# Query and key of two of eight batches transposed by DMA instead of VectorE

## The chip, the cores and the metric

The kernel runs on one core of one Trainium2 chip. The metric is the device time of one execution in microseconds (us); the median of three runs of the kernel before is 153.43 us (152.05 to 155.81). A core has five engines with a queue of instructions each: TensorE (PE, matrix products into PSUM; its weight loads are shown as PEld), VectorE (DVE), ScalarE (ACT), GpSimd (POOL) and SyncE (SP). POOL and SP also issue DMA transfers; all transfers run on the same 16 DMA engines. Each engine works through its own instructions in the order in which they were written, and waits on semaphores for the others.

## The reference

The inputs are `q`, `k` and `v`, each of 8 batches, 8 heads, 576 positions and 64 elements in float32, and the weights of a highway layer of width 512.

```python
rel = pos[:, None] - pos[None, :]
scores = q @ k.T / sqrt(64) + slope[h] * (-abs(rel))      # slope[h] = 2 ** -(h + 1)
scores = where((rel >= 0) & (rel < 128), scores, -1e9)    # causal window of 128
x = softmax(scores) @ v                                   # -> 4608 rows of 512 (8 heads x 64)
H = relu(x @ w_h);  T = sigmoid(x @ w_t + b_t)
out = T * H + (1 - T) * x
```

The output is float32, 4,608 rows of 512. Inside the kernels the products run on bfloat16, cast by the loading DMAs.

## The kernel before, in words

**Units and blocks.** Attention goes by units `(b, s, g)`: batch b (8), half of the heads s (2, four heads each), half of the positions g (2): 32 units. The highway layer goes by blocks of 128 output rows `(b, i)`, 36 in all: four per batch, and in each odd batch a fifth (`i == 4`) with the first 64 rows of two batches.

**The order is written out by hand.** The string `ORDER` (L26) holds one letter per step, and `by` (L56) says which unit, block or load each next use of a letter takes; a digit behind a letter is the PSUM bank. Every step's instructions stand in their engines' queues in exactly this order. `LOADS` (L18) is the order of the loads among themselves.

**Steps of a unit.** `L` issues a load from POOL (L126 to L144): a `t` load brings q or k of four heads of a batch, cast to bfloat16, as 128 rows of 1,152 elements; a `v` load brings 128 positions of v for 8 or 16 heads in pieces of 64 elements. A load's semaphore is one of eight in rotation, so that each issue also waits for the load eight places earlier. `T` (L188) transposes a `t` tile on DVE in 32x32 blocks of pairs of elements, so that the 64 elements of a head stand in 32 rows as two interleaved halves. `s` (L197) makes the scores of a unit from them: products over 32 rows, two of them (e = 0, 1) added up in PSUM for each head and place, with the tiles of four heads at rows 0, 32, 64 and 96. `e` is the exponential on ACT (L245), `m` the multiplication with a table of bias and mask on DVE (L250); for three units, `MASK_PE` (L23), TensorE adds the bias to the scores instead (L204). `p` multiplies with v (L261 to L282; the sum of the probabilities comes along as a 65th column), and `n` divides, on DVE (L295, L296).

**Steps of a block.** `x` transposes x on TensorE, `c` copies it out on ACT, `h` is the product with `w_h` (L331). `u` gives relu(h) - x on DVE, in one instruction out of PSUM (L346) or, for the blocks in `RELU_ACT` (L15), after a relu on ACT (`r`, L338) from SBUF (L343). `z` is the product with `w_t` plus a product of a matrix that is one in its first row with the bias tile (L354, L356); for the blocks in `BIAS_ACT` (L20) ACT writes the bias into PSUM first (`w`, L360) and `y` adds the product (L364). `a` is tanh of half of it on ACT (L369), turned into the sigmoid by `t` on ACT (L373) or, for blocks in `GATE_DVE` (L16), by `k` on DVE (L377). `g` multiplies on DVE (L382). `o` adds x on POOL (L386), or `q` on DVE (L391) for the blocks in `ADD_DVE` (L21). `d` stores from SP (L394). The tiles `uu`, `tt` and `ot` have four buffers each.

So POOL's queue holds the loads and the sums of L386 in one order, SP's the stores, and a step that waits holds up all that stands behind it on its engine.

Of the kernel before, what the change touches and what calls it, by code (L numbers as in the profile page):

```python
# [9 lines left out]
P = 128  # L10
NB, NS, NG = 8, 2, 2
NLD, NTR, NPB = 20, 12, 8

RELU_ACT = (0, 3, 5, 8, 9, 11, 12, 13, 17, 19, 20, 21, 26, 28)  # L15
GATE_DVE = (6, 7, 9, 15, 19, 23, 25, 26, 29, 32, 34)  # L16

LOADS = (0, 1, 3, 4, 6, 5, 2, 12, 11, 9, 13, 17, 10, 16, 8, 18, 7, 14, 21, 19, 15, 20, 22, 27, 26, 23, 25, 24, 29, 30, 31, 32, 33, 28, 34, 37, 39, 35, 40, 47, 38, 36, 43, 44, 45, 46, 48, 42, 41, 52, 56, 57, 50, 53, 58, 59, 51, 49, 55, 54)  # L18

BIAS_ACT = (8, 9, 14, 17, 20, 24, 30, 31, 32, 33, 34, 35)  # L20
ADD_DVE = (33, 35)  # L21

MASK_PE = (11, 14, 19)  # L23
# [3 lines left out]
    "SLLSSLLLTLLTLs0LTLeLLTLSms0Lp4LeLTLmLs0LTp6enLs0nLmx4Lex5Tp6cmcs0Lnz4eLTp6mas0tnz4eLh5mx"  # L27
    "6rh7cux5az6ucgtTp4oaSp6nLds0nLh4Th5eLx6x7uLrs0Tcz4Leumh5cmx6as0cuz7egTp4oh6anLtds0Lmrp4t"
    "Luez6ngz7gaoTtx6p4aLmdcs0x7eh6noTp4Ltds0cLnmh7euz4kw6gux5aos0Tch7eLdTp4Lynrs0akmp4w7eyug"
    "nh6oaTx4rs0LdtgLcgLp6gmx4Lz5cnex4oTp6cLds0unLz4eoTp6aLds0anoh5tTeh4dmz6rux7ah4kmcx5tp6uc"  # L30
    "gs0rnox5ez4TLdh6gLcmax7s0roTz5cw4Lgp6deuTyLts0naLaLgz4ueLTop6Tas0otdh5enh4dgux6oth7ucgx4"
    "w5dh6mctoyurTx4ap6dcms0z4euknh5agp6Ttos0th4neLduz6rmLLx7ap4mcs0np6egx4kh5nocs0ruLdx4gw5p"
    "6LmcyeuLnh4Tox6az7rmtLdp4ags0cgz7otneTz6odTx4aLds0cx5mah4w7uh6cgkeuyoup4gtds0maz6eonx7Tp"
    "4dcs0nh7eTh4h5autmp6rgs0uz5oenx4mdp6cs0uakz4engx5p6macs0onx4z5cdmeh4ggp6aoux5nh4odctz5kr"
    "mdw4h6gauox7tx5uycgdkh6gaocx4h7ucodw6p4utydnw7ygagow6p4aytnodh7agdtx6ox4uh5ckw7dh6gcuoyw"
    "5uygdaqh4akdgtuogdqd"
# [3 lines left out]
def lists():  # L40

    units = [(b, s, g) for b in range(NB) for g in range(NG) for s in range(NS)]
    blocks = []
    for b in range(NB):
        blocks += [(b, 0), (b, 1)] + ([(b, 4)] if b % 2 else []) + [(b, 2), (b, 3)]
    trs = [(b, s, w) for b in range(NB) for s in range(NS) for w in range(2)]
    loads = []
    for b in range(NB):
        n = 1 if b < 2 else 2
        vs = [("v", b, n, m) for m in range(5)] if b < 2 or b % 2 == 0 else []  # L50
        ts = [("t", b, s, w) for s in range(NS) for w in range(2)]
        if b == 0:
            loads += ts[:2] + vs[:1] + ts[2:] + vs[1:3] + [("w", 0), ("w", 1), ("w", 2)] + vs[3:]
        else:
            loads += ts[:2] + vs[:3] + ts[2:] + vs[3:]
    by = dict(L=[loads[i] for i in LOADS], T=trs, S=list(range(5)))  # L56
    by.update({k: units for k in "sepn"})
    by["m"] = [u for i, u in enumerate(units) if i not in MASK_PE]
    by["pe_mask"] = [units[i] for i in MASK_PE]
    by.update({k: blocks for k in "xchuzagod"})  # L60
    by["w"] = by["y"] = [blocks[i] for i in BIAS_ACT]
    by["z"] = [bk for i, bk in enumerate(blocks) if i not in BIAS_ACT]
    by["q"] = [blocks[i] for i in ADD_DVE]
    by["o"] = [bk for i, bk in enumerate(blocks) if i not in ADD_DVE]
    by["r"] = [blocks[i] for i in RELU_ACT]
    by["k"] = [blocks[i] for i in GATE_DVE]
    by["t"] = [bk for i, bk in enumerate(blocks) if i not in GATE_DVE]
    return by
# [3 lines left out]
def kernel(  # L72
# [35 lines left out]
    ft = ctx.enter_context(tc.tile_pool(name="ft", bufs=4))  # L108
    pp = ctx.enter_context(tc.tile_pool(name="ps", bufs=1, space=PSUM))
# [4 lines left out]
    PB = [cp.tile([P, 4, 448], BF16, name=f"p{i}") for i in range(NPB)]  # L114
    wH = cp.tile([P, NC, DM], BF16, name="wH")
    wT = cp.tile([P, NC, DM], BF16, name="wT")
    bT = cp.tile([P, DM], BF16, name="bT")
    ident = cp.tile([P, P], BF16, name="ident")
# [7 lines left out]
    def load(kind, *at):  # L126
        if kind == "t":
# [3 lines left out]
                in_=(q, k)[w][b, 4 * s : 4 * s + 4].rearrange("h (p t) d -> (h p) (t d)", t=NT))  # L131
        elif kind == "v":
            b, n, m = at
            rows, h = min(P, S - m * P), b % 2 * H
            nc.gpsimd.dma_start(  # L135
                out=VA[b // 2][0:rows, h : h + n * H, m, 0:D],
                in_=v[b : b + n, :, m * P : m * P + rows].rearrange("b h p d -> p (b h) d"))
        elif at[0] < 2:
            nc.gpsimd.dma_start(
                out=(wH, wT)[at[0]][:],  # L140
                in_=(moe_w_h, moe_w_t)[at[0]].rearrange("(c p) n -> p c n", p=P))
        else:
            nc.gpsimd.dma_start(
                out=bT[:], in_=moe_b_t.rearrange("(o n) -> o n", o=1).to_broadcast([P, DM]))  # L144

    def setup(part):
        if part == 0:
            for i in range(NB // 2):
                nc.vector.memset(VA[i][:, :, :, D:E], 1.0)
            nc.vector.memset(PS[D:P, 0:4, 0:D], 0.0)  # L150
            nc.vector.memset(ones0[:], 0.0)
            nc.vector.memset(ones0[0:1, :], 1.0)
            nc.vector.memset(ident[:], 1.0)
        elif part == 1:
            rel = cp.tile([P, 256], I32, name="rel_i")
            far = cp.tile([P, 256], F32, name="far")
# [37 lines left out]

    PT, AV, X, SB = {}, {}, {}, {}

    def scores(b, s, g, bank):  # L197
        SB[b, s, g] = bank
        QT, KT = (TR[(4 * b + 2 * s + w) % NTR] for w in range(2))
        first = (b, s, g) not in by["pe_mask"]  # L200
        if not first:
            w = width(g)
            for a in range(4):
                nc.tensor.matmul(out=PS[:, bank + a, 0:w], lhsT=SI[:, 4 * s + a, :],  # L204
                                 rhs=RB[:, 448 - w : 448] if g else RB[:], start=True,
                                 stop=False, skip_group_check=True)
        for i in (2 * g, 2 * g + 1):
            lo, col = P * i, 192 * i - 448 * g
            for e in range(2):
                for r in range(2):  # L210
# [6 lines left out]
                    for a in range(4):  # L217
                        rows = slice(32 * a, 32 * a + 32)
                        nc.tensor.matmul(  # L219
                            out=PS[r * D : r * D + D, bank + a, c0:c1],  # L220
                            lhsT=KT[rows, lo + r * D : lo + r * D + D, e],
                            rhs=QT[rows, q0 : q0 + c1 - c0, e],
                            start=first and e == 0, stop=e == 1, tile_position=(32 * a, r * D),
                            skip_group_check=True)
# [3 lines left out]
        for e in range(2):  # L228
            for a in range(4):
                rows = slice(32 * a, 32 * a + 32)  # L230
                nc.tensor.matmul(  # L231
                    out=PS[0:D, bank + a, col : col + D],
                    lhsT=KT[rows, t * D : t * D + D, e], rhs=QT[rows, t * D : t * D + D, e],
                    start=False, stop=e == 1, tile_position=(32 * a, 0), skip_group_check=True)
# [64 lines left out]

    XP, XT, PA, PZ, TT, UU, OT = {}, {}, {}, {}, {}, {}, {}  # L300
# [56 lines left out]

    def bias(b, i, bank):
        PZ[b, i] = PS[:, bank, :]
        nc.scalar.copy(out=PZ[b, i], in_=bT[:])  # L360
# [33 lines left out]
    def store(b, i):  # L394
# [5 lines left out]
        for r in range(2):  # L400
# [3 lines left out]
    do = dict(L=load, T=tr, S=setup, s=scores, e=soft, m=mask, p=pv, n=norm, x=x_tr, c=x_copy,  # L404
              h=mm_h, u=relu_sub, z=mm_z, a=tanh, t=to_gate, k=to_gate_v, r=relu, g=gate, o=add_x, d=store,
              w=bias, y=mm_y, q=add_x_v)
    at = dict.fromkeys(by, 0)
    steps = iter("".join(ORDER))
    with tc.manual_schedule():
        for step in steps:  # L410
# [3 lines left out]
            if step in "spxhzw":  # L414
# [33 lines left out]
```

## Time and profile before

| | us |
|---|---|
| median of three runs | 153.43 |
| profiled execution, its own time | 152.83 |
| profiled execution, span from first to last instruction | 151.1 |
| TensorE busy | 124.7 |
| VectorE busy | 132.2 |
| ScalarE busy | 120.6 |
| GpSimd busy | 88.8 |
| 32 transposes on VectorE (L190), each | 1.249 |
| 32 exponentials (L245), mean of both widths | 1.560 |
| issue of a v load on POOL (L135), mean | 1.014 |
| issue of a q load on POOL (L129), mean | 0.579 |

The granted TensorE clock was 0.999 of full speed. The profile comes from one execution. Busy times are unions of an engine's instructions; a busy TensorE is not TensorE at its peak, since products are pipelined and their ends are modelled. The row of 40 slices shows for each slice of the span the busy share in tenths. A DMA share over 1 means that packets of several transfers were under way on an engine at once. A line of the chain has its start, its length and the instruction or transfer that the end of the kernel hung on at that time. A group's line has source line, engine and operation, the tiles, how often, busy time and mean.

### The profile page before, as it was taken

What the parts mean: (1) busy time and instruction counts of PE and PEld (TensorE: products, weight loads), DVE (VectorE), ACT (ScalarE), POOL (GpSimd) and SP (SyncE); (2) the same over time, 40 slices, a digit from 0 to 9 for tenths busy, and PEclk for the clock granted to TensorE, in tenths of its full rate; (3) what the DMA queues carried; (4) which work ended last, traced back from release to release, by engine and by line L of the source; (5) the groups of instructions that cost most, each with busy time, mean ns of one, the idle gap of its engine ahead of it and who ended that gap; (6) DMA issues with size and microseconds to landing.
All of it is one profiled execution on the core that took longest, in us unless ns stands there. A gap on an engine that the chain in (4) does not pass through costs nothing.

```text
span 151.1 us, 5746 instructions
## 1 busy us (share of the span) xinstructions
PE 124.7 (83%) x2485; PEld 79.6 (53%) x2516; DVE 132.2 (87%) x223; ACT 120.6 (80%) x182; POOL 88.8 (59%) x102
## 2 busy tenths in 40 slices
PE   0026587999999699979999989997999999999960
PEld 0026453656666356656655546674557566556520
DVE  4873995699998999999979999999999999976882
ACT  3559364798999589769999978989799888899860
POOL 6976753139276941996069970849656034675640
PEclk9999999999999999999999999999999999999999
DMA  2999999999999999999999999299999121343444
GB/s 37 186 159 174 188 199 200 179 193 180 149 123 206 218 207 187 170 140 174 258 233 203 137 210 297 47 184 209 163 230 149 73 78 50 86 148 139 188 144 157
DMA packets 48345, 25.14 MB, mean 166 GB/s; under 512 B 38464, under 2 KB 39616, under 8 KB 48320
## 3 DMA queue, kind: packets, MB, share of 16 engines
q0 software_dynamic: 43072, 15.34, 96.4%
q1 hardware_dynamic: 5248, 9.44, 18.4%
q8 instruction: 19, 0.31, 0.8%
q14 instruction: 6, 0.05, 0.1%
HBM read 30.67 MB, written 9.44 MB: 265 GB/s over the span
## 4 chain that ended last, share of the span: by engine, by line
PE 43%; DVE 25%; DMA 18%; POOL 7%; issue 3%; ACT 2%; POOLq 0%; DVEq 0%; ACTq 0%
PE ps L331 12%; PE ps L354 9%; DMA wT<-in_moe_w_t_dram 7%; DMA ld<-in_q_dram 6%; DVE p L250 6%; PE ps L364 5%; DVE x L296 5%; DMA va<-in_v_dram 5%; DVE tr L190 4%; PE ps L219 4%; POOL va L135 4%; PE ps L282 4%; PE ps L321 3%; DVE uu L382 3%; DVE uu L346 3%
## 5 line engine op out<-in xcount | busy, mean ns | idle before, releaser
L386 POOL TENSOR_TENSOR ot<-uu,x 128x512 f32<-128x512 bf16 x34 | 43.6, 1288 | 47.6 <-DVE uu L382 27.7
L245 ACT ACTIVATE p<-ps 128x1792 bf16<-128x1792 f32 (+1 forms) x32 | 49.9, 1560 | 12.6 <-PE ps L231 12.5
L190 DVE STREAM_TRANSPOSE tr<-ld 128x576 uint32<-128x576 uint32 x32 | 39.5, 1249 | 7.2 <-DMA ld<-in_q_dram 5.1
L331 PE MATMUL ps<-wH,xt 128*128 128x512 bf16 x132 | 34.9, 380 | 0.7 <-issue 0.2
L250 DVE TENSOR_TENSOR p<-p,mt 128x1792 bf16<-128x1792 bf16 (+1 forms) x29 | 30.0, 1041 | 1.3 <-ACT p L245 1.3
L219 PE MATMUL ps<-tr,tr 32*64 32x192 bf16 (+1 forms) x1024 | 18.4, 259 | 11.2 <-DVE tr L190 10.9
L135 POOL DMA_DIRECT2D va<-in_v_dram x25 | 25.2, 1014 | 2.6 <-DMA ld<-in_q_dram 2.0
L354 PE MATMUL ps<-wT,xt 128*128 128x512 bf16 x80 | 23.9, 389 | 2.1 <-DMA wT<-in_moe_w_t_dram 0.9
L296 DVE TENSOR_TENSOR x<-ps,rd 128x512 bf16<-128x512 f32 (+1 forms) x32 | 24.3, 758 | 1.3
L369 ACT ACTIVATE tt<-ps 128x512 f16<-128x512 f32 x36 | 21.5, 604 | 4.4 <-PE ps L356 2.7
L326 ACT COPY xt<-ps 128x512 bf16<-128x512 bf16 x36 | 21.0, 586 | 3.3 <-PE ps L321 3.1
L331 PEld LDWEIGHTS <-xt 128*128 128x128 bf16 x144 | 13.0, 98 | 13.1
L219 PEld LDWEIGHTS <-tr 32*64 32x64 bf16 x1024 | 11.7, 111 | 15.0 <-DVE tr L190 11.1
L261 PE MATMUL ps<-va,p 128*128 128x65 bf16 x256 | 14.1, 200 | 4.9 <-DVE x L296 2.2
L261 PEld LDWEIGHTS <-p 128*128 128x128 bf16 x256 | 12.0, 102 | 9.8 <-DVE p L250 3.1
L346 DVE SCALAR_TENSOR_TENSOR uu<-ps,x 128x512 bf16<-128x512 f32 x22 | 14.9, 684 | 1.9 <-PE ps L331 1.8
L382 DVE TENSOR_TENSOR uu<-uu,tt 128x512 bf16<-128x512 bf16 x36 | 15.9, 454 | 0.2
L373 ACT ACTIVATE tt<-tt 128x512 f16<-128x512 f16 x25 | 15.7, 634 | 0.1
L321 PE MATMUL ps<-ident,x 128*128 128x128 bf16 x144 | 13.9, 225 | 2.1 <-DVE x L296 1.8
L282 PE MATMUL ps<-va,p 64*64 64x65 bf16 x448 | 14.9, 202 | 0.0
L321 PEld LDWEIGHTS <-x 128*128 128x128 bf16 x144 | 10.2, 99 | 8.8 <-issue 2.3
L354 PEld LDWEIGHTS <-xt 128*128 128x128 bf16 x96 | 8.3, 98 | 9.0 <-issue 1.7
(46 smaller groups left out, 129.5 us busy)
## 6 DMA issues: line engine op xcount, KB each, us to landing
out_dram<-ot SPq DMA_DIRECT2D x32, 256.0 KB, 4.2
ld<-in_q_dram POOLq DMA_DIRECT2D x16, 288.0 KB, 7.9
ld<-in_k_dram POOLq DMA_DIRECT2D x16, 288.0 KB, 7.2
va<-in_v_dram POOLq DMA_DIRECT2D x12, 256.0 KB, 7.4
va<-in_v_dram POOLq DMA_DIRECT2D x11, 128.0 KB, 9.4
out_dram<-ot SPq DMA_DIRECT2D x8, 128.0 KB, 3.3
wT<-in_moe_w_t_dram POOLq DMA_DIRECT2D x1, 512.0 KB, 10.8
wH<-in_moe_w_h_dram POOLq DMA_DIRECT2D x1, 512.0 KB, 12.2
```

Source lines behind the costliest of these rows:

```text
L135: nc.gpsimd.dma_start(out=VA[b // 2][0:rows, h : h + n * H, m, 0:D], in_=v[b : b + n, :, m * P : m * P + rows].rearrange("b h p d -> p (b ...
L190: nc.vector.transpose(out=TR[i % NTR][:].rearrange("p s e -> p (s e)").bitcast(U32).rearrange("p (s t) -> p t s", t=NT), in_=LD[i % NLD][: ...
L219: nc.tensor.matmul(out=PS[r * D : r * D + D, bank + a, c0:c1], lhsT=KT[rows, lo + r * D : lo + r * D + D, e], rhs=QT[rows, q0 : q0 + c1 - ...
L245: nc.scalar.activation(out=PB[i][:, :, 0:w], in_=PS[:, bank : bank + 4, 0:w], func=ACTF.Exp, scale=scale)
L250: nc.vector.tensor_tensor(out=p[:, :, 0:w], in0=p[:, :, 0:w], in1=MT[s][:, :, 448 - w : 448] if g else MT[s][:], op=ALU.mult)
L261: nc.tensor.matmul(out=PS[:, bank + o, a * E : a * E + E], lhsT=p[:, a, col : col + P], rhs=VA[b // 2][:, b % 2 * H + 4 * s + a, i, :], st ...
L296: nc.vector.tensor_tensor(out=X[b, g][:, s, :, 0:n, :], in0=av[:, :, 0:n, 0:D], in1=rd[:, :, 0:n, :].to_broadcast([P, 2, n, D]), op=ALU.mult)
L321: nc.tensor.transpose(out=XP[b, i][:, c * P : (c + 1) * P], in_=xchunk(b, i, c), identity=ident[:])
L331: nc.tensor.matmul(out=pa, lhsT=XT[b, i][:, c, :], rhs=wH[:, c, :], start=c == 0, stop=c == NC - 1)
L354: nc.tensor.matmul(out=pz, lhsT=xt[:, c, :], rhs=wT[:, c, :], start=c == 0, stop=False)
L369: nc.scalar.activation(out=tt[:], in_=PZ.pop((b, i)), func=ACTF.Tanh, scale=0.5)
L386: nc.gpsimd.tensor_tensor(out=like(ot[:], i), in0=like(UU.pop((b, i))[:], i), in1=xview(b, i), op=ALU.add)
```

## The change

For batches 6 and 7 (`XB`), q and k take another way. A `c` load casts all eight heads of a batch's q or k into a tile in DRAM with 576 rows of 512 bfloat16 elements (4 loads in place of 8 `t` loads). A new step `X` issues from SP two DMA transposes of 576 rows by 128 columns each from there into a tile `QK`, which holds two heads in 128 rows, 64 rows each (8 steps, 16 transposes, in place of 8 transposes on DVE). The score products of these units run over 64 rows, with no second half to add: 20 products in place of 40 per unit.

The bias row is loaded into one row of its tile instead of being repeated over 128; step `b` spreads it by a product with the matrix that is one in its first row, and `f` copies it for ACT's use (`bB`). There are 15 load buffers instead of 20, and two tiles of the setup lie in probability buffers. `ORDER`, `LOADS` and the lists that say which engine does a block's step are new: `RELU_ACT` has 9 entries instead of 14, `GATE_DVE` 17 instead of 11, `BIAS_ACT` 13 instead of 12, `ADD_DVE` 3 instead of 2, `MASK_PE` 3 as before.

```diff
-NLD, NTR, NPB = 20, 12, 8
+NLD, NTR, NPB = 15, 12, 8
+XB = (6, 7)
...
+        if b in XB:
+            ts = [("c", b, w) for w in range(2)]
...
+    SC = {(b, w): dp.tile([S, DM], BF16, name=f"sc{b}{w}") for b in XB for w in range(2)}
+    QK = {(b, w): cp.tile([P, 4, S], BF16, name=f"qk{b}{w}") for b in XB for w in range(2)}
...
+        elif kind == "c":
+            b, w = at
+            nc.gpsimd.dma_start(out=SC[b, w][:].rearrange("t (h d) -> t h d", d=D),
+                                in_=(q, k)[w][b].rearrange("h t d -> t h d"))
...
-            nc.gpsimd.dma_start(
-                out=bT[:], in_=moe_b_t.rearrange("(o n) -> o n", o=1).to_broadcast([P, DM]))
+            nc.gpsimd.dma_start(out=bT[0:1, :], in_=moe_b_t.rearrange("(o n) -> o n", o=1))
...
+            nc.vector.memset(bT[:], 0.0)
...
-            rel = cp.tile([P, 256], I32, name="rel_i")
-            far = cp.tile([P, 256], F32, name="far")
+            rel, far = (PB[i][:].rearrange("p a n -> p (a n)")[:, 0:512] for i in (6, 7))
+            rel, far = rel.bitcast(I32), far.bitcast(F32)
...
+    def dma_tr(b, s, w):
+        for j in (2 * s, 2 * s + 1):
+            nc.sync.dma_start(out=QK[b, w][:, j, :], in_=SC[b, w][:, j * P : (j + 1) * P],
+                              transpose=True)
...
+        def products(r, c0, c1, k0, q0, e, start):
+            for a in range(4):
+                if wide:
+                    row = D * (a % 2)
+                    lhsT = KT[row : row + D, 2 * s + a // 2, k0 : k0 + D]
+                    rhs = QT[row : row + D, 2 * s + a // 2, q0 : q0 + c1 - c0]
+                else:
+                    row = 32 * a
+                    lhsT = KT[row : row + 32, k0 : k0 + D, e]
+                    rhs = QT[row : row + 32, q0 : q0 + c1 - c0, e]
+                nc.tensor.matmul(
+                    out=PS[r * D : r * D + D, bank + a, c0:c1], lhsT=lhsT, rhs=rhs, start=start,
+                    stop=wide or e == 1, tile_position=(row, r * D), skip_group_check=True)
...
-            for e in range(2):
+            for e in range(1 if wide else 2):
...
+    def bias_rows(bank):
+        PB0.append(PS[:, bank, :])
+        nc.tensor.matmul(out=PB0[0], lhsT=ones0[:], rhs=bT[:], start=True, stop=True)
+
+    def bias_copy():
+        nc.scalar.copy(out=bB[:], in_=PB0[0])
...
-        nc.scalar.copy(out=PZ[b, i], in_=bT[:])
+        nc.scalar.copy(out=PZ[b, i], in_=bB[:])
```

In the new order the casts of batch 6 stand at steps 292 and 299 of 634, those of batch 7 at 340 and 419; the transposes of batch 6 at 335 to 363, those of batch 7 at 385 and 462 to 473; the first score unit of batch 6 at 402, that of batch 7 at 492. In the old order of 640 steps these two units stand at 407 and 488. Loads of v for batches 6 and 7 stand between the casts of batch 7.

## The prediction

> **What bounds the kernel now.** I read the shares first, then the rows of the span, then busy time by stretch, the chain, and last the landing of each load.
>
> ```profile
> PE 124.7 (83%) x2485; PEld 79.6 (53%) x2516; DVE 132.2 (87%) x223; ACT 120.6 (80%) x182; POOL 88.8 (59%) x102
> ...
> DVE  4873995699998999999979999999999999976882
> ...
> DMA  2999999999999999999999999299999121343444
> ...
> q0 software_dynamic: 43072, 15.34, 96.4%
> q1 hardware_dynamic: 5248, 9.44, 18.4%
> ```
>
> VectorE (DVE) is the fullest engine. The DMA row is at 9 until the last load has landed (117.5 us) and low after it. So two resources are full together, and the change takes work from one and gives it to the other. Busy time by stretch (columns: PE, weight loads, DVE, ACT, POOL, clock, DMA share, GB/s):
>
> ```profile
> 30.00:130.00 100.00, 94.35 (x2014) 60.55 (x2039) 96.60 (x159) 88.65 (x130) 59.93 (x61) 1.00 1.26 170
> 75.00:117.00 42.00, 39.79 (x842) 25.16 (x851) 40.57 (x69) 38.93 (x55) 28.57 (x28) 1.00 1.30 189
> 117.00:151.10 34.10, 28.51 (x434) 16.86 (x440) 27.65 (x54) 25.10 (x40) 14.88 (x12) 0.99 0.34 118
> ```
>
> From 30 to 130 us DVE idles 3.4 us in 100. TensorE's 94.35 contains the latency of short products, so it is less full than it looks: a 512-column product shows 380 ns but follows its neighbour after 216. After 117 us DMA is nearly free and PE sets the pace (28.5 us up to 146). The chain shows what a late load costs:
>
> ```profile
> 33.73 4.24 POOL va L135 x4
> 37.97 9.44 DMA ld<-in_q_dram
> 47.44 1.26 DVE tr L190
> ```
>
> Four loads of v were issued ahead of a load of q; it landed 9.4 us after its issue and DVE took it up at once.
>
> **What a load costs the queue.** Where the queue is full, landings follow each other at the price of one load. Loads of q and k (128 pieces of 4,608 bytes): 1.40, 1.41, 1.38, 1.44 us. Loads of v of 1,024 pieces of 256 bytes: 0.89, 0.91, 0.96, so 0.90 ns a piece, 1.8 us for 2,048 pieces (1.9 to 2.5 seen, with stores between). Stores of 256 KB one after another: 0.58 to 0.63.
>
> **The change, part by part.**
>
> DVE. Eight transposes go: 8 x 1.249 = -10.0. Five blocks go from relu on ACT to the fused form: 5 x (0.684 - 0.480) = +1.0. Six more gates: 6 x 0.300 = +1.8. One more final sum: +0.7. The memset of the bias tile: +0.25 (a quarter of its size took 0.165). One masked unit is a wide one: 0.946 - 1.118 = -0.2. Net **-6.4** of 132.2.
>
> ACT: 5 relus x 0.603 and 6 gates x 0.634 go (-6.8); one more bias copy and the one that makes the bias row cost 2 x 0.6. Net **-5.6**.
>
> PE. A score unit of 40 products takes 0.53 to 0.60 us. Its 20 products of 64 rows: the nearest row is the 64*64 product of L282, 16 in 0.37 us, 23 ns each, so 0.46. Ends: at 13 ns each (the present pace) 0.27; streamed two at a time, 3,072 columns x 0.42 ns / 2 = 0.65. For eight units -2.2 to +0.8; I take -0.8. Bias products nearly cancel (one fewer, one more).
>
> POOL. A final sum (1.29) and eight issues of 0.567 go. Issues cost 0.55 us at 128 pieces, 0.91 at 1,024 and 1.18 at 2,048, that is 0.29 us per 1,000 pieces more, so 1.9 for a cast of 4,608. Net 7.6 - 5.8 = +1.8, covered by 40% idle; without that cover the sums of L386 and all later loads move by it.
>
> Queue, casts. A cast reads 64-element pieces like v's, 8 x 576 = 4,608 of them, and writes DRAM, which no row shows. Below: it reads 1.18 MB, twice a q load, 2.8 us. By v's rate 4.15. Above: each piece paid for as a read and again as a write, 8.3. I take 4.15 as v's row has the same pieces and cast; four cost 16.6 where eight loads cost 11.2: **+5.4**. The Trainium skill (DMA: Bandwidth & Descriptors, Specifications) says that below 512 bytes a write becomes a read-modify-write; v's rows already write 128 bytes each to SBUF at 0.90 ns, so no run here shows that cost in DRAM.
>
> Queue, transposes. Each of 16 reads 576 pieces of 256 bytes: 0.52 us by v's rate. Below: 147 KB at the q loads' rate of 0.42 MB/us, 0.35; above: 4,608 short pieces to write, 4.15. I take 0.52: **+8.3**. The same page (Latency and other measured facts) gives DMA transposes 261 GB/s; an estimate by that is 0.56 each, 9.0 in all, which no run here shows.
>
> SP. A transpose waits for its cast, and the stores behind it wait too. Who waits for them: a final sum that needs one of four output buffers, and behind it on POOL the next loads. At most two stores stand directly behind the first transposes; with four buffers I cost that at nothing, up to 3 us if a cast is 5 us late.
>
> Covered edits: 15 load buffers instead of 20 suffice, since the loads that reuse them need transposes that end by 33.7 us, and the first reuse is issued about then. Setup values in two probability buffers are done by 8 us; those buffers are first written at 35.6. The bias load of one row saves a landing step of 0.44 early, which I take as 0. The new start order has the second weight tile behind the same loads, so the same 28 us.
>
> **Sum on engines alone.** DVE's -6.4 in a stretch where it is 96.6% busy is worth at most 6.6 us. The chain is on DVE for some 38 of those 100 us and on PE otherwise: at least 0.38 x 6.6 = 2.5. I take 4.4, so a span of 146.7.
>
> **Sum on the queue.** The last load of batches 4 and 5's v landed at 88.6 with the queue full from 65.7 on. Now two q loads fewer lie ahead (-2.8) and it is issued 24 steps of 640 earlier (some 5 us): I take 83. Between it and the first score unit of batch 7 the queue must carry four casts 16.6, v of batches 6 and 7 4 x 1.8 + 0.9 = 8.1, twelve transposes 6.2 and ten stores 6.0: 36.9, and the last transfer lands 1.7 us after issue even on a free queue (the last stores do). So that unit starts near **121.6**. Before it stood at 116.96; by the engine sum it would stand at 116.96 - 4.4, plus 2.6 for one block and one value unit that now stand ahead of it: 115.2. So it is 6.4 us late, and behind it in PE's order stand all products of the tail. The tail was 34.1 us; without that block and unit 31.5, with cheaper scores 31.1. Span 121.6 + 31.1 = 152.7.
>
> The profiled execution of before took 152.83 against a span of 151.1: 1.7 more. So **154.4**, against 152.83 and a median of 153.43: what DVE gains, the queue takes back.
>
> **Rivals.**
>
> *The queue keeps up.* The casts are ready before PE asks, the engine sum holds: 146.7 + 1.7 = 148.4, between 146.2 and 150.3. For: the queue has holes now, the 0.2 in its row near 95 us among them, and my 36.9 leaves no overlap of stores and loads, though shares over 1 show two packets in flight. Against: 36.9 us of transfers would have to pass in the 32 us from 83 to 115.2, where the old kernel moved eight q or k loads, six whole v loads' worth and eleven stores, some 29 us by the same prices, in the 37 us from 80.5 to 117.5.
>
> *DRAM writes of 128 bytes are dear.* This ends on the other side. If a cast costs 8.3, four add 16.6, all ahead of the first unit of batch 7: 171. Halfway, at 6.2, 162.7. It is slower by more than 2% from (156.5 - 154.4) / 4 = 0.5 us over my price, i.e. 4.7 a cast. For: the write side of a piece goes to another memory than any in the trace. Against: writes may hide behind reads, as v's do. The read-modify-write of the Trainium skill (DMA: Bandwidth & Descriptors, Specifications) would give this case. Transposes above 0.7 us each do the same.
>
> *The 64-row products bring nothing on PE:* then PE gains 0 instead of 0.8, +0.4 us in the tail.
>
> **Chances.** Forecast with its own range of 150 to 159: 0.42. Queue keeps up: 0.28. Dear writes or transposes, 157 to 171: 0.30. A time between 150.4 and 156.5 is within 2% of the median, about what a measurement here can tell from no change. The forecast's range gives 0.04 to faster, 0.28 to same, 0.10 to slower; the first rival 0.26 and 0.02; the second all to slower but 0.01. So faster 0.30, same 0.31, slower 0.39. The range that leaves 0.2 out reaches from 147.5 to 165.
>
> **What would show it.** Casts: landing steps near 4 us in a full queue; 6 or more means dear writes. Transposes: landing steps near 0.5 us. The first score unit of batch 7 near 121 with PE idle before it, waiting for a transpose; near 115 without a wait if the queue keeps up. DVE busy near 126, ACT near 115. DMA row at 9 beyond 117. The prediction is wrong if PE waits for no transposed tile, or if the loss comes from POOL's issues or from stores held on SP.

## The result

The changed kernel takes a median of **164.88 us** (163.75 to 166.78) against 153.2 (152.05 to 155.81) for the kernel before on the same chip. The ratio is **1.0825, 95% interval 1.0765 to 1.0885: slower**. The forecast was 154.4 with a range of its own of 150 to 159, and the time lies outside it; it lies in the rival case that had 0.30 (dear writes or dear transposes, 157 to 171), just inside the widest range named, 147.5 to 165. All ratios leave out the executions that took over 1.5% more than the fastest of their kernel. The profiled execution took 165.2 us with a span of 163.5, where the forecast had 152.7.

### The profile after

The page of the changed kernel: busy time, the rows of the span in 40 slices of 4.1 us, and the queues.

```profile
span 163.5 us, 5470 instructions
...
PE 129.9 (79%) x2356; PEld 80.3 (49%) x2356; DVE 131.5 (80%) x223; ACT 117.1 (72%) x173; POOL 93.4 (57%) x97
...
PE   0027779999999969999999997329969499999960
...
PEclk9999999999999999999999999955899999999996
DMA  3999999999999999999999998999996687313336
...
q0 software_dynamic: 60304, 15.21, 110.5%
q1 hardware_dynamic: 14976, 11.80, 27.7%
```

The reader is to see three things. The row of DMA stays at 9 until 124 us; before it ended at 117. TensorE (PE) has a hole at 102 to 110 us and idles again at 119 and from 128 to 131, ahead of the first unit of batch 7. And behind the first hole the granted clock falls to near half, which it did in no slice of the page before. The second queue (q1), with the transposes, carries 9,700 packets more than before, the first (q0), with the casts, 17,200 more.

Busy time by stretch (PE, weight loads, VectorE = DVE, ScalarE = ACT, GpSimd = POOL, clock, DMA share, GB/s):

```profile
30.00:130.00 100.00, 87.04 (x1676) 53.78 (x1674) 85.06 (x140) 74.36 (x101) 61.31 (x53) 0.95 1.68 174
...
97.00:103.60 6.60, 5.23 (x69) 2.81 (x67) 5.17 (x9) 3.83 (x5) 6.37 (x6) 1.00 1.44 169
103.60:109.80 6.20, 0.44 (x7) 0.17 (x10) 3.82 (x5) 1.41 (x3) 4.98 (x4) 0.68 2.28 145
109.80:116.20 6.40, 6.40 (x96) 4.51 (x97) 2.70 (x6) 3.78 (x5) 3.06 (x3) 0.51 1.53 229
```

From 103.6 to 109.8 PE does 0.44 us of work in 6.2: it waits for the transposed tiles of the second unit of batch 6. In the 6.4 us behind that it is always busy, at half clock.

The chain that ended last, between 76 and 136 us (start, length, what the end hung on):

```profile
77.59 9.80 DMA sc<-in_q_dram
...
87.41 1.22 SPq L211
...
88.68 1.91 SPq L211
...
90.68 6.37 DMA out_dram<-ot
...
97.22 1.16 POOL ot L420
...
102.12 2.29 POOL va L149 x2
104.41 1.18 POOL ot L420
105.59 0.75 POOL va L149
106.34 18.68 DMA sc<-in_k_dram
...
125.04 1.15 SPq L211
...
126.23 1.26 SPq L211
...
132.45 2.79 DMA qk<-sc
...
135.29 0.50 PE ps L241 x16
```

This is the change as a chain. A cast is awaited (9.80); two transposes take SP 3.1 us; the store behind them lands 6.4 us after its issue; a sum on POOL waited for that store's buffer; behind the sum stand the loads of v and the last cast, issued at 106.34; that cast needs 18.68 us in a full queue; and its transposes take SP once more. The waits (total, times, longest) and the transposes' own line (min, median and max in ns) say the same:

```profile
POOL ot L420 <- DMA out_dram<-ot: 13.3, 4, 5.9
...
PEld L241 <- DMA qk<-sc: 9.3, 4, 4.2
```

```profile
L211 SPq DMA_TRANSPOSE qk<-sc x16: 1145/1270/2848, 87.4 to 132.5; - x16
```

A store takes SP 0.33 us, a transpose 1.27.

### The profile page after: what moved, and what is told of

Same layout as the page of the kernel before. It is cut to its first block, busy times and chain, and to the rows that moved or that the text cites. A ratio compares the mean times of both kernels' runs of the same rounds, so it can differ in the third digit from the quotient of the medians.

```text
span 163.5 us, 5470 instructions
## 1 busy us (share of the span) xinstructions
PE 129.9 (79%) x2356; PEld 80.3 (49%) x2356; DVE 131.5 (80%) x223; ACT 117.1 (72%) x173; POOL 93.4 (57%) x97
## 4 chain that ended last, share of the span: by engine, by line
DMA 33%; PE 20%; DVE 20%; POOL 8%; SPq 6%; issue 5%; ACT 4%; DVEq 0%; POOLq 0%
DMA sc<-in_k_dram 11%; DMA va<-in_v_dram 10%; DMA sc<-in_q_dram 6%; SPq L211 6%; PE ps L358 5%; DVE tr L204 5%; DVE x L322 4%; POOL va L149 4%; DMA out_dram<-ot 4%; DVE p L276 4%; PE ps L308 3%; POOL ot L420 3%; PE ps L241 3%; DVE uu L373 3%; PE ps L287 2%
## 5 line engine op out<-in xcount | busy, mean ns | idle before, releaser
L358 PE MATMUL ps<-wH,xt 128*128 128x512 bf16 x144 | 39.1, 397 | 1.4 <-DVE uu L373 1.4
L276 DVE TENSOR_TENSOR p<-p,mt 128x1792 bf16<-128x1792 bf16 (+1 forms) x29 | 31.0, 1071 | 0.5 <-ACT p L271 0.5
L204 DVE STREAM_TRANSPOSE tr<-ld 128x576 uint32<-128x576 uint32 x24 | 29.3, 1248 | 2.4 <-DMA ld<-in_k_dram 1.4
L241 PE MATMUL ps<-tr,tr 32*64 32x192 bf16 (+2 forms) x960 | 16.0, 251 | 12.4 <-DVE tr L204 11.8
L381 PE MATMUL ps<-wT,xt 128*128 128x512 bf16 x92 | 23.7, 380 | 0.0
L373 DVE SCALAR_TENSOR_TENSOR uu<-ps,x 128x512 bf16<-128x512 f32 x27 | 18.5, 685 | 6.0 <-PE ps L358 3.3
L241 PEld LDWEIGHTS <-tr 32*64 32x64 bf16 x960 | 12.9, 114 | 17.2 <-DVE tr L204 11.9
L358 PEld LDWEIGHTS <-xt 128*128 128x128 bf16 x144 | 12.7, 100 | 13.7 <-issue 3.3
L321 DVE RECIPROCAL rd<-ps 128x8 f32<-128x8 f32 (+1 forms) x32 | 6.6, 205 | 15.6 <-PE ps L308 15.4
L416 DVE TENSOR_TENSOR uu<-uu,tt 128x512 bf16<-128x512 bf16 x36 | 17.2, 485 | 0.2
L398 PE MATMUL ps<-wT,xt 128*128 128x512 bf16 x52 | 13.4, 379 | 0.0
```

The source lines that it names most:

```text
L204: nc.vector.transpose(out=TR[i % NTR][:].rearrange("p s e -> p (s e)").bitcast(U32).rearrange("p (s t) -> p t s", t=NT), in_=LD[i % NLD][: ...
L241: nc.tensor.matmul(out=PS[r * D : r * D + D, bank + a, c0:c1], lhsT=lhsT, rhs=rhs, start=start, stop=wide or e == 1, tile_position=(row, r ...
L276: nc.vector.tensor_tensor(out=p[:, :, 0:w], in0=p[:, :, 0:w], in1=MT[s][:, :, 448 - w : 448] if g else MT[s][:], op=ALU.mult)
L358: nc.tensor.matmul(out=pa, lhsT=XT[b, i][:, c, :], rhs=wH[:, c, :], start=c == 0, stop=c == NC - 1)
L373: nc.vector.scalar_tensor_tensor(out=like(uu[:], i), in0=like(PA.pop((b, i)), i), scalar=0.0, in1=xview(b, i), op0=ALU.max, op1=ALU.subtract)
L381: nc.tensor.matmul(out=pz, lhsT=xt[:, c, :], rhs=wT[:, c, :], start=c == 0, stop=False)
```

## The experiments

After the result there were three candidates. **Queue**: transposes (and casts) fill the transfers' time. **Hold**: SP stands in transposes, stores come late, and POOL holds back loads. **Order**: the forecast's gain was not there in the first place, whatever the DMA path costs. All times below are medians; without a ratio beside it a time is that of one execution, and the kernel before took 151.8 to 152.5 beside all of them. None of the kernels beats the kernel before by more than its interval while it does the whole work.

### Parts of the change, undone or left out

**All by the old path, in the new order.**

```diff
-XB = (6, 7)
+XB = ()
-NLD, NTR, NPB = 15, 12, 8
+NLD, NTR, NPB = 20, 12, 8
```

> The changed kernel with one part undone: q and k of batches 6 and 7 come by the old loads, are transposed on VectorE at the places where the DMA transposes stood, and their scores are 32-row products; 20 load buffers. New order, bias row and choice of engines stay. If the loss of 12 us sits in casts and DMA transposes (theories 'hold' and 'queue'), the time falls back to 148 to 156 us, VectorE busy near 141. If the new order or the other choices are to blame (theory 'order'), it stays above 160 us.

Measured: 163.24, as the theory 'order' expected. The new order with VectorE's transposes in it is nearly as slow as with the DMA path: it holds its time only with a VectorE that does not have them.

**No transposes, large constant tiles.**

```diff
-    "...Xs0anoh6...
+    "...s0anoh6...
+            for t in list(QK.values())[2 * s : 2 * s + 2]:
+                nc.vector.memset(t[:], 0.01)
```

> The changed kernel without its 16 DMA transposes; the tiles that they filled are set to a constant at the start (so the scores of batches 6 and 7 are not those of the inputs); the four casts stay in the queue. Theory 'hold' (the transposes hold SP's queue, the stores behind them come late, output buffers stay taken, POOL's sums and with them the later loads wait): the 13.3 us that sums waited for stores vanish, 147 to 151 us. Theory 'queue' with the casts as its main load: the v loads of batches 6 and 7 still land 5 us or more later than in the kernel before, 154 to 160 us.

Measured: 162.57, but the four fills of these tiles delay the first score unit from 8.3 to 12.3 us, and the time is spoilt by that. It was made again with one tile of 192 columns.

**Stores between the transposes issued from ACT.**

```diff
+        eng = nc.sync if at["X"] == 0 or at["X"] == 8 and b > 5 else nc.scalar
-            nc.sync.dma_start(out=out[row : row + P, :], in_=ot[:])
+            eng.dma_start(out=out[row : row + P, :], in_=ot[:])
```

> The changed kernel with the stores from the first to the last transpose issued from ScalarE instead of SP, so that no store stands behind a transpose; all transfers stay. Theory 'hold': sums no longer wait for stores, v of batch 6 and the last cast are issued some 8 us earlier, 154 to 158 us. Theory 'queue' (the transfers themselves fill the DMA engines): first unit of batch 7 at 126 us or later as now, 162 to 166 us.

Measured: 167.98. The stores left SP, but ACT now shows 11.3 us of waits that end when a transposed tile lands. A new wait took the place of the old, so this run decides nothing about "hold".

**One cast, which all 16 transposes read.**

```diff
-            nc.sync.dma_start(out=QK[b, w][:, j, :], in_=SC[b, w][:, j * P : (j + 1) * P],
+            nc.sync.dma_start(out=QK[b, w][:, j, :], in_=SC[6, 0][:, j * P : (j + 1) * P],
```

> The changed kernel with one cast (q of batch 6) in place of four; all 16 transposes read its tile (so the scores of batches 6 and 7 are not those of the inputs). It takes 12.4 us of casts out of the queue and leaves all transposes on SP. Theory 'queue': v of batch 6 lands by 112 us, 150 to 155 us. Theory 'hold': stores still stand behind 1.27 us a transpose and the sums still wait for them, 158 to 163 us.

Measured: 158.55, in the range of 'hold'. Scores are those of other data. Three casts fewer are worth 6.3 us; the sixteen transposes are all still there.

**Casts without transposes, one small constant tile of 128 x 192 (`QC`); and the same without casts.**

```diff
-            QT, KT = (QK[b, w] for w in range(2))
+            QT = KT = QC
```

> The changed kernel without its 16 DMA transposes, with the four casts left in the queue. The scores of batches 6 and 7 are made from one small constant tile of 128 x 192 (so they are not those of the inputs), set at the start in about 0.2 us, in place of the four large tiles whose setting cost e2_no_transposes some 4 us at its start. Theory 'transposes' (the loss of the change sits in the DMA transposes: SP held, packets in the queue): 153 us or less. Theory 'order' (even with the data there in time the new order runs no faster): 156 to 160 us, first unit of batch 7 near 120 us.

> As e6_casts_alone, and the four casts left out as well: nothing of the DMA path of batches 6 and 7 is left but the 64-row products, on constants. What remains is the new order with its choice of engines, relieved of eight transposes on VectorE. By the engine sum of the prediction 146 to 150 us. If it stays above 153 us, the new order loses the relief by itself. The difference to e6_casts_alone is what the casts cost: theory 'queue' says 4 us or more, theory 'transposes' under 1.5 us.

Measured: 157.43 with the casts; 153.23 without them (156.16 in a second execution). So the new order, with the path for free, is at best where the kernel before is. The casts add 4.2 us to the lower time and 1.3 to the other, which leaves their cost open. It is not the queue alone. Around the last cast of the run with casts (VectorE, then POOL; start, length):

```profile
103.41 5.30 DVE L277 TENSOR_TENSOR p<-p,mt 128x1536 bf16<-128x1536 bf16 x1
```

```profile
102.27 2.24 POOL L144 DMA_DIRECT2D sc<-in_k_dram  x1
103.99 3.89 POOL L421 TENSOR_TENSOR ot<-uu,x 128x512 f32<-128x512 bf16 x3
```

A multiplication that takes 0.95 us elsewhere takes 5.30 while POOL issues the cast and runs three sums without a pause. PE idles for 4 us meanwhile, and then runs at half clock:

```profile
104.75:108.75 4.00, 0.00 (x0) 0.00 (x0) 4.00 (x2) 1.63 (x3) 3.13 (x3) 0.83 2.15 185
108.75:114.25 5.50, 4.64 (x57) 3.29 (x58) 4.13 (x8) 1.13 (x3) 0.00 (x0) 0.50 1.20 197
```

**The old order with the DMA path.** Old `ORDER`, lists and bias; the casts stand where room was, the transposes where VectorE's stood or later.

```diff
-RELU_ACT = (0, 4, 5, 7, 13, 16, 28, 31, 34)
+RELU_ACT = (0, 3, 5, 8, 9, 11, 12, 13, 17, 19, 20, 21, 26, 28)
...
-LOADS = (0, 1, 3, 4, 11, ...)
+LOADS = (0, 1, 3, 4, 6, ...)
```

> One part alone: the order, the choice of engines and the bias row of the kernel before, and only batches 6 and 7 by cast, DMA transpose and 64-row products. Casts are issued where loads of q and k stood (steps 221, 291, 317, 389 of the old order), each pair of transposes right behind a store and at least 14 steps ahead of its scores. If DMA path and VectorE's relief of 10 us work when the transfers are early, 146 to 151 us and first unit of batch 7 near 113 us. If the queue cannot carry casts and transposes beside the v loads, that unit starts after 120 us and the time is 156 us or more.

Measured: 167.34, ratio 1.094 (1.0841 to 1.104). Casts put earlier push the loads behind them: a load of v that landed at 75.3 us in the kernel before lands at 81.1, and the unit that started at 75.2 starts at 82.0 (in an execution of 168.9). So an earlier cast is no cure while the queue is full.

### What a transpose costs

**Plain copies in place of transposes: 128 pieces of 1,152 bytes, and in another kernel 512 of 256 bytes.**

```diff
-            nc.sync.dma_start(out=QK[b, w][:, j, :], in_=SC[b, w][:, j * P : (j + 1) * P],
-                              transpose=True)
+            nc.sync.dma_start(
+                out=QK[b, w][:, j, :],
+                in_=SC[b, w][j * 144 : (j + 1) * 144, :].rearrange("r c -> (r c)").rearrange(
+                    "(p n) -> p n", p=P))
...
+            nc.sync.dma_start(
+                out=QK[b, w][:, j, 0:512].rearrange("p (r c) -> p r c", c=P),
+                in_=SC[b, w][0:512, j * P : (j + 1) * P].rearrange("(p r) c -> p r c", p=P))
```

> The changed kernel with each DMA transpose replaced by a plain copy of the same 147 KB in pieces of 1,152 bytes from the same DRAM tile into the same tile, with the same waits for the casts (rows are not transposed, so the scores of batches 6 and 7 are not those of the inputs). If the transposes' own cost decides (1.27 us of SP each, 576 small packets), SP is held a quarter as long and the time comes near that of e6_casts_alone, within 2 us. If it is the waiting for the casts that holds SP and PE, it stays within 3 us of the changed kernel, 161 to 165 us.

> The transposes become plain copies again, now in pieces of 256 bytes, 512 per copy (the transposes have 576 of that size; the last 64 columns are filled with a constant at the start, so the scores are other ones). The copies in pieces of 1,152 bytes took 158.3 us. Theory 'packets' (the number of short pieces in the queue is what costs): 162 to 165, near the changed kernel. Theory 'transposing' (what costs is that a piece is transposed: 1.8 times the queue of a plain piece, and 1.27 us of SP for each issue): 157.5 to 160, since 16 x 512 plain pieces at 0.83 ns are 6.8 us where the longer pieces were about 5.6.

Measured: 158.26 and 158.83 (ratio 1.044, 1.0385 to 1.0494). Copies in pieces of the same size, 512 of them in place of 576, cost 6 us less than the transposes. It is the transposing, not the short pieces.

**SP's time without the queue's.** A second copy of 128 bytes behind each short-piece copy.

```diff
+            nc.sync.dma_start(out=TINY[0:1, w, j, :], in_=SC[b, w][0:1, j * P : j * P + 64])
```

> The plain copies in 256-byte pieces (158.8 us) with a second, tiny copy of 128 bytes behind each of the 16: SP spends on each pair about the 1.27 us that it spends on a transpose, and the queue gets next to nothing more. Theory 'SP time' (a transpose costs because SP is taken for 1.27 us and stores stand behind it): 163 to 165. Theory 'queue' (a transposed piece weighs more in the queue than a plain one): 158.5 to 160.5.

Measured: 161.04, ratio 1.0547 (1.0464 to 1.0629). What the pairs take on SP (min, median and max in ns):

```profile
L214 SPq DMA_DIRECT2D qk<-sc x16: 523/530/1277, 87.2 to 127.6; - x16
L217 SPq DMA_DIRECT2D tiny<-sc x16: 467/472/795, 87.8 to 128.2; - x16
```

The time lies between the two expectations: SP's time alone costs about 2 of the 6 us. That is a rough figure, since this interval and that of the plain copies overlap, and a pair takes 1.00 us of SP where a transpose takes 1.27. It works by "hold": in the profiled execution (162.0) POOL's wait for stores is 9.5 us where it was 3.9, and the last cast is issued at 105.5 in place of 102.6.

**Half of them transposed.** q as short plain copies, k transposed.

```diff
+            if w == 0:
+                nc.sync.dma_start(out=QK[b, w][:, j, 0:512]..., in_=...)   # plain
+            else:
                 nc.sync.dma_start(out=QK[b, w][:, j, :], in_=..., transpose=True)
```

> The changed kernel with q as plain copies in 256-byte pieces and k transposed: 8 transposes in place of 16. Both theories on the transposes expect the middle between 158.8 and 164.9 us, 161 to 163, if each transpose costs alike; a time near 159 or near 165 would mean that a single one of them decides (the first, or those behind the last cast).

Measured: 163.75, ratio 1.0632 (1.053 to 1.0733), which is 161.9 by the ratio. The ratio rests on two executions, of 160.8 and 162.7; all four scatter from 160.8 to 165.3. They fit a middle, but do not exclude that single transposes weigh more than others.

**Transposes behind the stores on SP.**

```diff
-    "op4uLdx6nh7tLcmp4rLs0w7unz6eLmp4as0nx6eygmp4aos0nch7tgex6oz4uTh5akch4gw7uox6XTrycLddp4ua"
-    "gs0mtz6eonXz7madXp4kgXs0anoh6edmLx7dp4cgus0ox7nh6cXLez7udLmh6ax7kLp4ucw6s0kgz7kenoygLdag"
+    "op4uLdx6nh7tLcmp4rLs0w7unz6eLmp4as0nx6eygmp4aos0nch7tgex6oz4uTh5akch4gw7uox6TrycLddp4uag"
+    "s0mtz6eonz7madXp4kgs0anoh6edXmLx7dXp4cgus0ox7nh6cLez7udXLmh6ax7kLp4ucw6s0kgz7kenoygLdXag"
...
```

> The changed kernel with its eight transpose steps moved on SP behind the next one or several stores; nothing else moves. Theory 'hold' (stores wait on SP behind transposes that wait for their cast, POOL then waits 13.3 us for output buffers and issues the loads of v and the last cast late): POOL's wait for stores falls under 6 us, the last cast is issued 3 to 8 us earlier than 106.3, and the time is 159 to 162. Theory 'queue' (the transposes take 0.86 us of the transfers' time each, wherever they stand): 164 to 166, with the wait moved to the products.

Measured: 167.74, ratio 1.1034 (1.0955 to 1.1112): slower still, and above both ranges. What "hold" asks for came, and the time did not fall. POOL's wait for stores, and the last cast's issue:

```profile
POOL ot L420 <- DMA out_dram<-ot: 2.1, 1, 2.1
```

```profile
101.97 2.24 POOL L144 DMA_DIRECT2D sc<-in_k_dram  x1
```

The cast is issued 4.4 us earlier than in the changed kernel and lands at 124.55 in place of 125.02. The queue decides when it lands. Behind that, new waits took the place of the old: the first unit of batch 7 has its main products 2 us earlier than in the changed kernel (128.7), but the second, whose transposes now stand behind stores, has them 0.7 us later (135.9), and the clock is halved from 137.0 to 140.4. So the run shows that "hold" does not set the landing, not that it costs nothing elsewhere.

This run also gives the weight of a transpose. From 100 to 116 us, with the queue full throughout, 7,611 pieces of v and casts (0.83 ns each where they run alone) take 6.3 us and 510 store packets (6.1 ns) 3.1; the 3,885 transposed pieces have the other 6.6, that is 1.7 ns each or **1.0 us for a transpose** of 576. The same count in the changed kernel from 105.2 to 114 gives 1.6 ns and 0.9 us. From 98 to 114 it would give 1.2 us, but there the queue stands nearly still from 98.0 to 98.8 and from 104.0 to 104.8: single pieces that take 0.03 us elsewhere take 0.7 to 1.6 us. All six traces with 16 transposes have such stretches, and none of the thirteen without transposes; what stops the pieces was not tried. The plain short pieces, from 92 to 104 in their run, have 1.3 ns, 0.75 us for 576.

The landings say the same without prices for the other packets. The last cast was issued at 102.0 in this run, at 102.3 in the run with casts alone and at 102.6 in the one with short plain copies. It landed at 124.6, 115.0 and 120.1: ten transposes ahead of it cost 9.5 us, 0.95 each, ten plain copies 5.1, 0.5 each.

### Where the gain went

**Loads of v ahead of q and k, without and with the path.** Only the sequence of the loads is changed: the last two loads of v of batch 2 move ahead of q and k of batch 4, and of the five of batch 4 three move ahead of one load of q or k each; its first moves behind two such loads, and its last stays. The diff has the loads by their names.

```diff
-LOADS = (..., t(3,0,1), t(3,1,1), v2, t(3,1,0), v2, v2, t(4,0,0), t(4,0,1), v2, v2, ...)
+LOADS = (..., t(3,0,1), t(3,1,1), v2, t(3,1,0), v2, v2, v2, v2, t(4,0,0), t(4,0,1), ...)
```

> The new order without casts and transposes (scores of batches 6 and 7 from a small constant tile, 153.2 us), with the loads of v for batches 2 and 4 ahead of the next batch's q and k; only the sequence of the loads is permuted, not their places. Theory 'late v' (the engine sum of the prediction is right, and v that lands late in the new order takes its gain): 147 to 150, and the chain shows no wait of 9 us or more on v. Theory 'engines' (the gain is not there, VectorE and POOL hold each other up and the freed time lies in front of PE): 152 to 154.

> The changed kernel with both edits: transposes behind the stores on SP, loads of v ahead. Theory 'hold' with 'late v': the two gains add up, 155 to 159. Theory 'queue': 163 to 166, since the queue has the same transfers in it whatever their sequence.

Measured: 155.16 (1.0197, 1.0127 to 1.0266) without the path, 169.89 (1.1169, 1.1085 to 1.1254) with it and with the transposes behind the stores. Both lie above every range that was given. Without the path the chain no longer shows long waits on v, and the time is no shorter. Late v was not the reason.

**The old order, with batches 6 and 7 from a constant.** The kernel before, with eight loads of q and k and eight transposes on VectorE left out.

```diff
-        QT, KT = (TR[(4 * b + 2 * s + w) % NTR] for w in range(2))
+        if wide:
+            QT = KT = QC
+        else:
+            QT, KT = (TR[(4 * b + 2 * s + w) % NTR] for w in range(2))
```

> The kernel before with its old order, lists and load sequence, in which batches 6 and 7 have no loads of q and k and no transposes; their scores come from a small constant tile as 64-row products. This is what a transpose by DMA could bring at most in the old order. Theory 'engine sum' (VectorE's ten microseconds bound the kernel, and the new order lost them again): 145 to 149. Theory 'no gain' (VectorE's transposes are covered by other work whatever the order): 151 to 153, like the 153.2 of the new order without the path.

Measured: 154.02, ratio 1.0125 (1.007 to 1.0179). Ten microseconds less on VectorE, with nothing to pay for them, make the kernel *slower* by one per cent. With two earlier runs this makes a square (us):

| | VectorE transposes batches 6, 7 | scores of 6, 7 from a constant |
|---|---|---|
| old order | 152.3 | 154.0 |
| new order | 163.2 | 153.2 |

The relief is worth 10 us in the new order (one time each) and nothing in the old one; the new order at its best is no better than the old one. In the old order with a constant, PE is busy without a gap from 75 to 105 us and from 120 to 135, the first 15 of them:

```profile
75.00:90.00 15.00, 15.00 (x291) 9.18 (x289) 14.03 (x25) 14.52 (x23) 9.06 (x8) 1.00 0.97 130
```

**What bounds it then? PE relieved, alone and with VectorE, then ACT too.** One of the four products with `w_t` is left out in every block (7.8 us of PE at 216 ns), in the kernel before and in the last run; then the sigmoid step on ACT is left out as well, for 12 blocks (7.6 us).

```diff
-        for c in range(NC):
+        for c in range(NC - 1):
...
     def to_gate(b, i):
+        if i % 2:
+            return
```

> The kernel before without the last of the four products with w_t in each of its 36 blocks: at the pace of 216 ns that is 7.8 us less of TensorE and nothing less of VectorE. Theory 'PE' (TensorE is as full as VectorE, so relieving one of them alone brings little): 149 to 153. Theory 'PE alone bounds' : 144 to 147. Theory 'VectorE alone bounds': 151 to 153.5.

> The old order without the path (154.0 us: VectorE relieved of 10 us, scores from a constant tile) and without the last of the four products with w_t. Theory 'PE' (both are full together, and only relieving both shows): 144 to 148, with PE idle again and the granted clock at 1.0 except behind idle times of over 2 us. Theory 'something else bounds' (late v, the loads' order, ACT): 151 to 154.

> As the run before it (old order, VectorE relieved of 10 us, TensorE of 7.8 us; 152.8 us), and ScalarE relieved too: for every block with an odd number the step that turns tanh into the sigmoid is left out (0.634 us each on ScalarE), so the gate of these blocks is another. Theory 'three together' (TensorE, VectorE and ScalarE are each over nine tenths full from 75 to 135 us, and only relieving all of them shows): 146 to 150. Theory 'the order' (each engine's queue was written for the old durations, and what one step gives is lost at the next wait of another engine): 151.5 to 153.5.

Measured: 151.13 (0.9965, 0.9927 to 1.0004), 152.83 (1.0063, 1.0025 to 1.01) and 152.27 (1.0028, 0.9985 to 1.0072). Taking 10, 7.8 and 7.6 us off three engines leaves the time where it was. Busy time by stretch of the run with VectorE and PE relieved, from 75 us on:

```profile
75.00:90.00 15.00, 14.11 (x286) 9.10 (x289) 14.69 (x27) 14.73 (x23) 9.07 (x8) 1.00 0.90 142
90.00:105.00 15.00, 14.51 (x315) 9.48 (x317) 13.19 (x23) 13.63 (x20) 7.83 (x7) 1.00 0.53 94
105.00:120.00 15.00, 12.52 (x193) 7.91 (x195) 11.28 (x21) 13.20 (x19) 8.03 (x7) 1.00 1.17 148
120.00:135.00 15.00, 14.35 (x227) 9.28 (x229) 14.73 (x29) 13.68 (x22) 7.03 (x6) 1.00 0.23 73
```

No engine is full in all four stretches: VectorE has 14.69 and 14.73 us of 15 in the first and the last, 11.28 in the third. The chain changes engine every microsecond or two, and a product that comes earlier waits for the next instruction of another engine in the written order. So the theory "three together" falls too. "Order" is what is left: it is argued and not shown, since no order was rewritten.

## Why the prediction was wrong

Half of its mechanism held: the queue delays the last cast, and PE stands idle before the first unit of batch 7 and waits for a transposed tile, as forecast. In "what DVE gains, the queue takes back" the queue term was too small, and the gain does not exist. In its own steps:

- **Last v of batches 4 and 5 at 83:** it landed at 83.14. Right.
- **Casts, 4.15 each:** the first two landed at steps of 4.25 and 3.82 us in a full queue. Right; the dear writes did not come. The read-modify-write of the Trainium skill (DMA: Bandwidth & Descriptors, Specifications) shows no cost here.
- **Transposes, "I take 0.52":** this step failed. A transpose weighs 0.9 to 1.0 us in the full queue, nearly twice that. The nearest row was v's, with the same piece size; it holds for plain copies to within a half, but not where the pieces are transposed. The upper bound of 4.15 was in the working, and the price of 0.7 from which the time is slower was named; the value taken was below it. The Trainium skill's 261 GB/s (DMA: Bandwidth & Descriptors, Latency and other measured facts) would be 0.56 for 147 KB; 0.9 to 1.0 us are 147 to 164 GB/s.
- **First unit of batch 7 at 121.6:** its first two products ran at 128.1, the rest at 130.6:

```profile
128.11 0.27 PE L241 MATMUL ps<-qk,qk 64*64 64x192 bf16 x1
...
130.62 0.52 PE L241 MATMUL ps<-qk,qk 64*64 64x192 bf16 x18 [2.14 <-DMA qk<-sc]
```

  The 9.0 us go apart like this. Ten of the twelve transposes stand ahead of the last cast; by the forecast's prices that makes 83 + 16.6 + 8.1 + 5.2 + 6.0 = 118.9 for the cast's landing, and it landed at 125.0, 6.1 late. Ten transposes at 0.95 in place of 0.52 are 4.3 of these. The other 1.8 have room in three stretches of 0.8 us, from 98.0, 100.8 and 104.0, in which few packets landed; the sum had no holes. From that landing to the main products it took 5.6 us and not 2.7: SP needs 2.4 us to issue two transposes one after the other, and the second lands 3.1 us later.
- **SP, "at nothing, up to 3 us":** POOL waited 13.3 us for output buffers. By the run with tiny copies, SP's time costs some 2 us. By the run with the transposes behind the stores, the cast lands no earlier without that wait. So the term was mis-sized, but is not the main one.
- **Tail, 31.1:** 32.9 from the unit's main products to the end. Together 9.0 + 1.8 = 10.8, which is the span's 163.5 against 152.7.
- **Net -6.4 on DVE:** its transposes lose 10.0 us, but gates on DVE take 416 ns and not 300 (17 of them: +3.8 in place of +1.8), the multiplication with the gate 485 and not 454 (+1.1), and the masks +0.9 in place of -0.2. The groups sum to -2.6, busy time to 131.5 against 132.2, not near 126. ACT fell by 3.5 and not 5.6. On POOL a cast's issue took 2.2 to 2.8 us and not 1.9, and busy time rose by 4.6, not 1.8.
- **"DVE's -6.4 ... is worth at most 6.6 us ... I take 4.4":** this step failed as well, without any harm to the total, as the queue sum was the later one. With the path free the gain is none, in either order. Reading 96.6% busy as a bound was the error: PE and ACT are over nine tenths busy from 75 to 117 us as well, and the relief of VectorE, of PE, of both or of all three brought next to nothing. Why is not settled beyond that.
- **Not in the sum: the clock.** PE idled 3.7 and 2.1 us at 103.6 to 109.8, and the granted clock was 0.50 from 105.8 to 116.1. PE worked in 6.7 us of that, so some 3.3 us of its work went there; what the span would be without it was not tried.

Of the rivals, the first ("the queue keeps up") is out by the chain and by the row of DMA. The second names the right resource, by its last sentence. "64-row products bring nothing": a unit of 20 products takes 0.5 us where one of 40 took 0.53 to 0.60, so eight of them bring at most the 0.8 us that was forecast.

## What to carry to other kernels

A resource that looks full in a busy row is worth its relief only if the written order can use it: leave the work out first, with nothing in its place, and see whether the time falls; here two runs of that kind, one in each order, showed that nothing was to be won. A transfer that also transforms is not priced by a plain one with the same pieces; keep the dear end of the bounds likely until a run has measured it, and count the issue itself (1.3 us here) for everything queued behind it.

## What the runs showed of the hardware

- **A transposing DMA** of 576 by 128 bf16 elements takes SP 1.27 us to issue and 0.9 to 1.0 us of a full queue; as many plain 256-byte pieces take 0.6 and 0.5 to 0.75. Beside transposes the queue stood nearly still for 0.8 us at a time, as counted above.
- **The granted clock is halved for 3.41 us, or a multiple, behind 3.41 us in which PE did little.** In the old order with a constant tile:

```profile
65.00:67.50 2.50, 0.14 (x4) 0.18 (x4) 2.46 (x4) 1.20 (x2) 2.50 (x5) 1.00 1.93 151
67.50:69.25 1.75, 1.75 (x70) 1.37 (x70) 1.75 (x2) 0.26 (x1) 1.67 (x3) 1.00 2.25 157
69.25:72.75 3.50, 3.50 (x69) 2.31 (x68) 3.25 (x6) 2.70 (x4) 0.00 (x0) 0.51 1.14 255
```

  Behind 2.4 us with hardly a product and 1.75 us of work come 3.5 us at half clock, while PE is busy. That is 1.7 us of PE's work in this execution. It is not why this kernel is slower than the one before: its execution with a granted clock of 1.000 took 153.44 us, and the kernel before 152.3. In the clock records of all 20 traces the stretches between two changes are whole multiples of 3.41 us (at half clock 3.41, 6.83 and 10.24). All 32 falls ahead of a kernel's end follow 3.41 us in which PE was busy for at most 0.53 of the time. The clock stayed at 1.0 behind 668 such stretches, and in 662 of these PE was busy for more than 0.53. So it counts how the idle time lies to these stretches: here 65.8 to 69.2 had 0.53, and the clock fell; in the run with PE relieved as well, the same wait lies across two stretches with 0.57 and 0.62, and it did not fall. The Trainium skill (TensorE: Matmul & The Clock Gate, Part 1: The HAM clock gate) tells of half clock after an idle window of about 3.4 us; the length agrees, but PE did not have to be idle for all of it here.
- **VectorE and POOL hold each other up.** The multiplication of 5.30 us above is the longest case (also 5.29 in the run with large constant tiles and 5.30 in the one with stores from ACT). One of 2.46 in place of 1.08 stands in the old order with a constant tile at 63.8 us, beside one sum on POOL from 64.1 to 65.3. The changed kernel shows it only up to 1.04 us over (a multiplication with the gate of 1.45 in place of 0.41). That POOL's sums are the cause was read from the traces, not tried. The Trainium skill (SBUF — State Buffer, SBUF: two separate sides) says that a VectorE instruction with two inputs in SBUF and a reading POOL instruction lock each other out for a whole instruction; in the longest case the hold outlasts one instruction of POOL: the multiplication ends at 108.71, 0.83 us after the last of three sums.
